# Block-sparse attention with an FFN behind it on one core: who makes the low halves of the weights, and scores of two units in one TensorE task

## The chip, the cores and the metric

The kernel runs on 1 core of one Trainium2 chip. The metric is device time in microseconds (us) of one execution. Engines are named as in the profile: PE is TensorE, PEld its weight loads, DVE is VectorE, ACT is ScalarE, POOL is GpSimd, SP is SyncE, which issues most DMAs.

## The reference

Four batches of eight heads, 768 positions, head dimension 64. Queries and keys are cut into 24 blocks of 32. A query block sees its neighbours, the first and the last block and three sampled blocks; the first and last query block see everything. The result goes through a feed-forward net.

```python
scores = scale * np.matmul(q, k.transpose(0, 1, 3, 2))
mask = np.abs(blk_i - blk_j) <= 1
mask = mask | (blk_i == 0) | (blk_j == 0) | (blk_i == n_blocks - 1) | (blk_j == n_blocks - 1)
...                                     # and three sampled key blocks for each query block
attn = softmax(np.where(mask, scores, -1e9))
x = np.matmul(attn, v)                  # to rows of 512: [3072, 512]
h = x @ w_in                            # [3072, 2048]
out = np.maximum(0.01 * h, h) @ w_out   # [3072, 512]
```

## The kernel before, in words

**Precision.** PE multiplies 16-bit numbers. Every operand is split into a scaled fp16 number (the high half) and an fp16 remainder (the low half), and a product is three matmuls: high by high, high by low, low by high.

**Work.** The 3072 rows are 12 items of 256 rows, three to a batch. An item has four tiles T of 64 queries (two query blocks), and a tile has four units, one for each pair of heads: 192 units, numbered by `u.n`, and two units that follow each other are a pair. A unit goes through: scores (`unit_scores`, L1165, eight matmuls of half-width tiles into one of the two PSUM banks `s`), minimum and mask (`unit_ttr`, L1189, DVE, which frees the bank), exponential (`unit_exp`, ACT), normalising (`pair_norm`, DVE), high half (`unit_high`, ACT, `pp<-p,r`), low half (`unit_split`, DVE, `pp<-p,r,pp`), transposition (`pt<-pp`: by PE for units below 16, by a transposing DMA after that) and the product with the values (`pair_av`, L1245, half-width tiles into the one bank `av`). `tile_evac` (L1263) takes the finished tile out of PSUM: ACT `avt`, DVE `xf`, ACT `x` (high), POOL `x` (low). T = 0 of each batch is the pair of query blocks that see all keys; it has two parts and reads `kt` and `v` directly. The other tiles read gathered copies `kg` (DVE and POOL) and `vg` (DMAs, two of them indirect from POOL).

**FFN.** An item has eight chunks. Chunk: 24 matmuls into one bank `h` (`ffn_h`), ACT `ht<-h` (0.01 h), DVE `ht<-h,ht` (maximum), DVE cast `g<-ht` (high), POOL `g<-ht,g` (low) (`ffn_act1`, `ffn_max`, `ffn_act2`, L1298 to L1311), 12 matmuls into the two banks `o` (`ffn_o`). Items 0 and 1 are "early": they go quarter by quarter, as parts of the weights become ready.

**Weights.** They come as float64 in eight parts: 0, 2, 4, 6 are quarters of `w_in`, 1, 3, 5, 7 quarters of `w_out`. Parts 0 to 5 are handled in two groups of 128x1024 numbers, parts 6 and 7 in four of 128x512. `decode` (L813) makes float32 of the float64 bits: one ACT and three DVE instructions. `finish` (L864) finds one scale for the part (PE squares, DVE), then makes the fp16 halves of each group: ACT the high half, and for the low half the table `wsplit` (L67) says how. With "p" ACT scales the float32 numbers in place and POOL subtracts; with "d" one DVE instruction does both:

```python
nc.scalar.activation(hi, g.d3, AF.Copy, scale=s[:, :1])
if CFG["wsplit"][g.part] == "p":
    nc.scalar.activation(g.d, g.d, AF.Copy, scale=s[:, :1])
    nc.gpsimd.tensor_tensor(out=lo, in0=g.d3, in1=hi, op=ALU.subtract)
else:
    nc.vector.scalar_tensor_tensor(out=lo, in0=g.d3, scalar=s[:, :1], in1=hi, op0=ALU.mult, op1=ALU.subtract)
```

Before, parts 0 to 5 are "p" and 6 and 7 "d".

**Order.** The program is recorded as tasks (class `Plan`, L183). The main loop walks over the units and calls, in the order of the letters in `CFG["ord"]`, the steps of several units; each gets a priority. A planner then plays the tasks through with costs written in `cost` (L466) and fixes one order of instructions for each engine; a `block` of matmuls is one task that nothing comes between. In the running program each engine works strictly in that order and waits on semaphores. All instructions that go through the recording layer carry the profile's line L451 (L461 in the changed kernel), so they are told apart by tile names.

Of the kernel before, what the change touches and what calls it, by code (L numbers as in the profile page):

```python
# [15 lines left out]
F32 = mybir.dt.float32  # L16
# [20 lines left out]
    "pe_t": 16,  # L37
    "passes": 4,
    "stay_ns": 2000.0,
    "kg_dma": 0,  # L40
# [26 lines left out]
    "wsplit": "ppppppdd",  # L67
# [114 lines left out]
class Plan:  # L182
# [283 lines left out]
def cost(eng, method, a, k):  # L466
# [45 lines left out]
def tile_block_sparse_attention_ffn(  # L512
# [69 lines left out]
    group = {"s": banks[:2], "o": banks[2:4], "h": banks[4:7], "av": banks[7:]}  # L582
    turn = dict.fromkeys(group, 0)
# [106 lines left out]
    assert 222 + 2 * P <= DM and 6 + 2 * NB * NR <= 150  # L690
    offs = cst.tile([1, NT - 1, 8], I32, name="offs")
# [3 lines left out]
    lane_m = cst.tile([P, NT - 1, SLOTS], F32, name="maskhalf")  # L695
# [104 lines left out]
    def load_w(g):  # L800
# [12 lines left out]
        def decode():  # L813
# [8 lines left out]
            nc.vector.scalar_tensor_tensor(  # L822
                out=d, in0=hi, scalar=-0x80000000, in1=d, op0=ALU.bitwise_and, op1=ALU.bitwise_or)
# [6 lines left out]
    def prep_weights():  # L830
# [33 lines left out]
        def finish(n, kind, gs):  # L864
            plan.prio = 1000.0 + 200 * CFG["wp"][gs[0].part]
            inv, s = scales(squares([g.d for g in gs], f"{kind}{n}", "w"), 1, f"{kind}{n}", keep=f"{kind}{n}", fl="w")
            invs[kind, n] = inv
            yield 1
            for i, g in enumerate(gs):
# [7 lines left out]
                else:  # L877
                    nc.scalar.activation(hi, g.d3, AF.Copy, scale=s[:, :1])
                    if CFG["wsplit"][g.part] == "p":
                        nc.scalar.activation(g.d, g.d, AF.Copy, scale=s[:, :1])  # L880
                        nc.gpsimd.tensor_tensor(out=lo, in0=g.d3, in1=hi, op=ALU.subtract)
                    else:
                        nc.vector.scalar_tensor_tensor(
                            out=lo, in0=g.d3, scalar=s[:, :1], in1=hi, op0=ALU.mult, op1=ALU.subtract)
                yield g.w
            if kind == "wo":
                pr = cst.tile([P, 1], F32, name=f"pr{n}")
                nc.vector.scalar_tensor_tensor(
                    out=pr, in0=invs["wi", n][:, :1], scalar=1.0 / GDOWN, in1=inv[:, :1], op0=ALU.mult, op1=ALU.mult)
# [30 lines left out]
        done.add("all")  # L920
        yield 1
# [71 lines left out]
    def prep_k(b, hp, rk):  # L993
# [32 lines left out]
        else:  # L1026
            for h in range(2):
                turned("h", kts[b][:, 2 * hp + h, :], k16.rearrange("p n l d -> p (n l d)")[:, h * S:(h + 1) * S],
                       "DVE" if h else "ACT")
# [59 lines left out]
    def gather_k(b, T):  # L1089
# [6 lines left out]
        if n0 < CFG["kg_dma"]:  # L1096
            nc.sync.dma_start(out=kg[:, :, :P], in_=kt[:, :, t0:t0 + P])
# [22 lines left out]
        nc.gpsimd.tensor_copy(  # L1120
# [43 lines left out]
    @levelled(lambda u: u.n + CFG["pr"][0])  # L1164
    def unit_scores(u):  # L1165
        i, c0 = u.k // 2, u.k % 2 * Q2
# [6 lines left out]
        u.nsc = nscale[key]  # L1173
        qs, qxs, _ = qstack[u.b, u.j, i]
# [70 lines left out]
    def pair_av(pr):  # L1245
# [4 lines left out]
        for u in pr.units:  # L1250
            require_v(u.b, u.hp, u.T)
# [78 lines left out]
    def ffn_out(it, t, po, qs):  # L1330
        key = (it.b, "all" if len(qs) == NQ else qs[0])
        if key not in betas:
            betas[key] = cst.tile([P, 1], F32, name=f"beta_{key[0]}_{key[1]}")
            nc.vector.tensor_tensor(out=betas[key], in0=undo[key[1]], in1=vscale[it.b][:, :1], op=ALU.mult)
# [211 lines left out]
    def split_step():  # L1546
        if pend_split:
# [6 lines left out]
            if pu.pi == 1:  # L1554
                pend_av.append((step + CFG["av_lag"], pu.pair))

    def av_step(now=False):
        if pend_av and (now or pend_av[0][0] <= step):
            pr = pend_av.popleft()[1]
            tlive[0] -= 2 * pr.units[0].parts  # L1560
            while evs and pr.hp == 0:
                ev_step()
            pair_av(pr)
            if pr.hp == NP - 2:
                vfree[0] += pr.T > 0
                evs.append((pr.n, tile_evac(pr)))
# [8 lines left out]
    for u in units:  # L1575
# [34 lines left out]
        if step == 0:  # L1610
            unit_scores(u)
        c = aq[0] if aq else None
        for w in CFG["ord"]:
# [7 lines left out]
            elif w == "S" and step + 1 < len(units):  # L1621
                unit_scores(units[step + 1])
# [110 lines left out]
```

## Time and profile before

| what | us |
|---|---|
| median of 3 runs | 844.78 (842.82 to 851.21) |
| the profiled execution's own time | 852.83 |
| its span, first to last instruction | 851.1 |
| PE busy / PEld / DVE / ACT / POOL in the span | 750.1 / 492.0 / 597.5 / 502.5 / 372.3 |

A row of the timeline has start, duration, engine, line, operation, out<-in, shape, count of merged instructions, and in brackets the idle time in front of it and who ended it. Rows of the windows have, for a stretch, the busy time of each engine, the granted PE clock (1.00 is full), and the DMAs' share and rate. A matmul's own duration contains its latency; where many follow each other, the start-to-start distance counts.

### The profile page before, as it was taken

The page shows a single profiled execution, that of the slowest core. Times are in us where ns is not written, and L with a number is a line of the kernel's source. Part 1 is how long each engine was busy: PE and PEld are TensorE (multiplying, and loading weights), DVE is VectorE, ACT ScalarE, POOL GpSimd, SP SyncE. Part 2 cuts the span into 40 slices and gives each one's busy share as a digit, 9 for nine tenths or more (in the row PEclk, how much of TensorE's full clock was granted, in tenths as well). Part 3 has the DMA queues.
Part 4 walks back from the last instruction along what each step waited for, and adds up shares of the span by engine and source line. Part 5 has one row for each costly group of instructions (what it writes and reads, how often), then busy time and mean ns, then how long its engine had stood idle before and what let it go on. Part 6 is the DMA issues. An engine that isn't in the chain of part 4 may idle for free. (4 is left out here: it accounts for less than half of the span.)

```text
span 851.1 us, 19895 instructions
## 1 busy us (share of the span) xinstructions
PE 750.1 (88%) x7204; PEld 492.0 (58%) x7204; DVE 597.5 (70%) x1642; ACT 502.5 (59%) x1087; POOL 372.3 (44%) x558
## 2 busy tenths in 40 slices
PE   3565656688979999999999999999999999979997
PEld 2353445455646656666665666656656666656674
DVE  5897699988768887878867577589587575662221
ACT  6779677566665665757647566476466464552111
POOL 0225457634323555554544446455435364532221
PEclk9567679689989999999999999999999999999999
DMA  9615966598797999999989989789568687591000
GB/s 189 230 39 173 331 149 196 137 192 183 136 150 165 202 206 194 173 213 179 218 163 158 204 152 214 149 160 226 127 130 174 119 157 129 104 165 25 13 14 25
DMA packets 305326, 133.28 MB, mean 157 GB/s; under 512 B 272205, under 2 KB 284621, under 8 KB 305229
## 3 DMA queue, kind: packets, MB, share of 16 engines
q1 hardware_dynamic: 299596, 114.71, 66.9%
q0 software_dynamic: 5632, 17.31, 9.5%
q8 instruction: 56, 0.92, 0.5%
q14 instruction: 42, 0.34, 0.1%
HBM read 65.65 MB, written 12.58 MB: 92 GB/s over the span
## 5 line engine op out<-in xcount | busy, mean ns | idle before, releaser
L451 PE MATMUL h<-x,W 128*128 128x256 f16 x2304 | 285.4, 280 | 8.6 <-ACT x L451 7.8
L451 PEld LDWEIGHTS <-W 128*128 128x128 f16 (+1 forms) x2480 | 240.2, 102 | 80.0 <-issue 24.3
L451 PE MATMUL o<-W,g 128*128 128x512 f16 x1152 | 272.1, 382 | 0.7 <-POOL g L451 0.7
L451 POOL TENSOR_TENSOR g<-ht,g 128x512 f16<-128x512 f32 x96 | 116.8, 1217 | 231.1 <-DVE g L451 182.3
L451 PEld LDWEIGHTS <-g 128*128 128x128 f16 x1152 | 107.4, 99 | 127.2 <-issue 16.6
L451 ACT ACTIVATE p<-p,mx 128x384 f32<-128x384 f32 x208 | 126.0, 607 | 68.8 <-DVE mx L451 66.7
L451 DVE SCALAR_TENSOR_TENSOR pp<-p,r,pp 128x384 f16<-128x384 f32 x208 | 143.4, 721 | 29.3 <-ACT pp L451 27.8
L451 ACT ACTIVATE pp<-p,r 128x384 f16<-128x384 f32 x208 | 117.6, 606 | 34.9 <-issue 11.9
L451 DVE SCALAR_TENSOR_TENSOR ht<-h,gd,ht 128x512 f32<-128x512 f32 x80 | 59.9, 748 | 94.7 <-ACT ht L451 94.3
L451 ACT ACTIVATE ht<-h,gs 128x512 f32<-128x512 f32 x80 | 54.6, 682 | 116.8 <-PE h L451 106.8
L1146 POOL DMA_INDIRECT vg<-scr,vrow x88 | 90.7, 1031 | 70.4 <-PE av L451 49.9
L451 DVE CUSTOM_DVE_ANT_0 p<-s,em,nsc 128x384 f32<-128x384 f32 x176 | 105.3, 609 | 22.7 <-PE s L451 21.5
L1111 POOL COPY kg<-kt 128x128 int32 x264 | 82.3, 348 | 69.2 <-PE s L451 55.3
L451 PE MATMUL av<-pt,vg 128*64 128x128 f16 x2112 | 83.0, 225 | 15.6 <-DMA pt<-pp 8.1
L451 PEld LDWEIGHTS <-vg 128*64 128x64 f16 x2112 | 67.2, 112 | 44.4 <-issue 33.3
L451 PE MATMUL s<-kg,qs 128*64 128x384 f16 x352 | 61.8, 346 | 9.6 <-DVE mx L451 4.2
L451 PE MATMUL s<-kg,qxs 128*64 128x384 f16 x352 | 60.8, 339 | 0.2 <-DMA qxs<-qs 0.2
L451 POOL TENSOR_TENSOR x<-xf,x 128x256 f16<-128x256 f32 x48 | 35.9, 748 | 34.3 <-ACT x L451 32.5
L451 DVE CAST g<-ht 128x512 f16<-128x512 f32 x96 | 42.8, 445 | 10.2 <-PE o L451 7.4
L451 PEld LDWEIGHTS <-qs 128*64 128x64 f16 x416 | 27.7, 113 | 34.9 <-issue 28.5
L451 ACT ACTIVATE avt<-av 128x256 f32<-128x256 f32 x48 | 18.1, 378 | 37.1 <-PE av L451 33.8
L451 ACT ACTIVATION_READ_ACCUMULATOR p<-p,mx 128x1 f32 x208 | 39.3, 189 | 0.0
(127 smaller groups left out, 765.5 us busy)
## 6 DMA issues: line engine op xcount, KB each, us to landing
vg<-scr SPq DMA_DIRECT2D x44, 256.0 KB
v<-in_v_dram SPq DMA_DIRECT2D x32, 192.0 KB
qxs<-qs SPq DMA_DIRECT2D x48, 128.0 KB
scr<-v SPq DMA_DIRECT2D x16, 384.0 KB
rq<-in_q_dram SPq DMA_DIRECT2D x20, 256.0 KB
W<-in_moe_w_in_dram SPq DMA_DIRECT2D x5, 1024.0 KB
out_dram<-ob SPq DMA_DIRECT2D x20, 256.0 KB
rk<-in_k_dram SPq DMA_DIRECT2D x24, 192.0 KB
```

Source lines behind the costliest of these rows:

```text
L451: self.plan.task(self.eng, lambda: f(*a, **k), busy, late, reads, writes, kind, loads, port)
L1111: tc.nc.gpsimd.tensor_copy(out=kg.ap.bitcast(I32)[:, :, slot * BLOCK // 2:(slot + 1) * BLOCK // 2], in_=kt.ap.bitcast(I32)[:, :, bass.ds(o ...
L1146: tc.nc.gpsimd.indirect_dma_start(into.ap, None, scr[b].ap, bass.IndirectOffsetOnAxis(ap=at.ap, axis=0))
```

## The change

1. `wsplit` becomes "ddeeeedd". The low halves of parts 0 and 1 are now made by DVE ("d"). Parts 2 to 5 use a new way "e": a diagonal matrix with the negated scale (`dg`) is made once for a part by ACT; for each 128x512 piece PE multiplies the float32 numbers by it (an f32 matmul) and adds the high half (an fp16 matmul with a unit matrix) in one PSUM bank, and ACT takes the bank out, negated, as the low half. Eight groups of two pieces: 16 such pairs of matmuls. The one bank for it is `h_69` (tag `wl`), taken from the three `h` banks until the last weight is done.
2. The cast `g<-ht` of items 0 and 1 (16 instructions) moves from DVE to ACT (`gact`).
3. From unit 48 on (`pair_at`), and except for T = 0, the scores of both units of a pair are one PE task, and if a `pair_av` is due at that step it is joined to the same task. `pair_av` is one task of 24 matmuls (it was two of 12). From there on a pair's value product comes due 5 steps after its split instead of 3 (`av_lag2`).
4. Small ones: the planner's cost of an f32 matmul is lower; `pr` and `beta` (one column each) are made by `tensor_scalar` instead of two-input forms; the scratch `lane_m` moves into another buffer; other new switches are off.

```diff
-    "wsplit": "ppppppdd",
+    "wsplit": 'ddeeeedd',
+    "pair_at": 48,
+    "join": 1,
+    "av_lag2": 5,
+    "gact": (0, 1),
...
     def block(self, eng="PE"):
+        if self.group is not None:
+            yield
+            return
...
         if lhs.dtype == F32:
-            return 60.0 + 4 * cols, 300.0 + 4 * cols, "f", []
+            return 60.0 + 4 * cols / 2.4, 300.0 + 4 * cols / 2.4, "f", []
...
+    if "e" in CFG["wsplit"]:
+        group["wl"], group["h"] = [group["h"][2]], group["h"][:2]
...
+            if CFG["wsplit"][gs[0].part] == "e":
+                neg = sm.tile([P, 1], F32, tag="neg", name=f"neg_{kind}{n}", bufs=2)
+                nc.vector.tensor_scalar(out=neg, in0=s[:, :1], scalar1=-1.0, scalar2=None, op0=ALU.mult)
...
-                    if CFG["wsplit"][g.part] == "p":
+                    if CFG["wsplit"][g.part] == "e":
+                        if not i:
+                            dg = cst.tile([P, P], F32, tag="dg", name=f"dg_{kind}{n}")
+                            nc.scalar.activation(dg, eye, AF.Copy, scale=neg[:, :1])
+                        for c in range(g.w):
+                            pb = bank("wl", "wl")
+                            with plan.block():
+                                nc.tensor.matmul(pb, dg, g.d3[:, c, :], start=True, stop=False)
+                                nc.tensor.matmul(pb, eye16, hi[:, c, :], start=False, stop=True)
+                            nc.scalar.activation(lo[:, c, :], pb, AF.Copy, scale=-1.0)
+                    elif CFG["wsplit"][g.part] == "p":
...
-        nc.vector.tensor_copy(out=c.g[:, 0], in_=c.t)
+        if c.item.n in CFG["gact"]:
+            nc.scalar.activation(c.g[:, 0], c.t, AF.Copy)
+        else:
+            nc.vector.tensor_copy(out=c.g[:, 0], in_=c.t)
...
+                elif nu.pi == 0:
+                    with plan.level(nu.n + CFG["pr"][0]):
+                        for x in nu.pair.units:
+                            before_scores(x)
+                    due = CFG["join"] and pend_av and pend_av[0][0] <= step
+                    if due:
+                        before_av(pend_av[0][1])
+                    with plan.level(nu.n + CFG["pr"][0]):
+                        with plan.block():
+                            for x in nu.pair.units:
+                                unit_scores(x)
+                            if due:
+                                pair_av(pend_av[0][1])
+                    if due:
+                        after_av(pend_av.popleft()[1])
```

The planner's orders differ nearly everywhere, since it fixes all of them anew. Three places matter below. On POOL, around the second item's first tiles (`x_220` before, `x_222` after, are the item's rows; `vg` gathered values, `offs` block numbers), there stands before:

```order
L451 TENSOR_TENSOR W<-W 128x2x512 x2
L451 TENSOR_TENSOR x_220<-xf,x_220 128x4x64
L1146 DMA vg_90<-scr_71,vrow 128x1024
L451 TENSOR_TENSOR W<-W 128x2x512 x2
L1081 TENSOR_LOAD offs
```

and now:

```order
L461 TENSOR_TENSOR g_217<-ht,g_217 128x512
L1184 DMA vg_89<-scr_71,vrow 64x1024
L1184 DMA vg_89<-scr_71,vrow 128x1024
L461 TENSOR_TENSOR x_222<-xf,x_222 128x4x64
L461 TENSOR_TENSOR g_221<-ht,g_221 128x512
L1114 TENSOR_LOAD offs
```

All twelve subtractions `W<-W` are gone from POOL. On ACT, at the high halves of part 2, there stands before:

```order
L451 ACTIVATE W<-kt_86 128x1024
L451 ACTIVATE W<-W,wi_s 128x2x512 x2
L451 ACTIVATE W<-W,wi_s 128x1024 x2
L451 ACTIVATE W<-W 128x1024
L451 ACTIVATE pp_141<-p_117,r_140 128x384
L451 ACTIVATE pp_142<-p_118,r_140 128x384
L451 ACTIVATE p_133,sum_148<-p_133,mx_119 128x384
L451 ACTIVATE avt<-av_70 128x256
```

and now:

```order
L461 ACTIVATE W<-W,wi_s 128x2x512 x2
L461 ACTIVATE dg<-eye,neg_199 128x128
L461 ACTIVATE p_132,sum_147<-p_132,mx_118 128x384
L461 ACTIVATE W<-W 128x1024
L461 ACTIVATE qa<-rq_106,sc_s_130 128x8x64
L461 ACTIVATE W<-h_69 128x512
L461 ACTIVATE p_133,sum_147<-p_133,mx_134 128x384
L461 ACTIVATE p_116,sum_161<-p_116,mx_144 128x384
L461 ACTIVATE W<-h_69 128x512
L461 ACTIVATE avt<-av_70 128x256
```

The two in-place scalings (`128x1024 x2` from `W,wi_s`) are gone; the pieces that PE has made are taken out one by one (`W<-h_69`) between the exponentials, and the tile's `avt` stands behind two of them. On PE, near unit 98 (first row of each run of matmuls; `s` scores, `av` value products, `h` and `o` FFN), there stands before:

```order
L451 MATMUL h_68<-x_220,W 128x256
...
L451 MATMUL av_70<-pt_143,vg_89 64x128
...
L451 MATMUL s_63<-kg_87,qs_173 64x384
...
L451 MATMUL s_64<-kg_87,qs_173 64x384
...
L451 MATMUL o_65<-W,g_219 128x512
...
L451 MATMUL av_70<-pt_153,vg_90 64x128
```

and now:

```order
L461 MATMUL h_68<-x_222,W 128x256
...
L461 MATMUL s_63<-kg_86,qs_172 64x384
...
L461 MATMUL s_64<-kg_86,qs_172 64x384
...
L461 MATMUL av_70<-pt_158,vg_88 64x128
...
L461 MATMUL av_70<-pt_142,vg_88 64x128
```

Two scores and a whole pair of value products now stand together. Over the whole program the change from full-width to half-width tiles and back happens 151 times in the order before and 121 times in the order now.

More of the change, by code (lines that the diff above doesn't have):

```diff
@@ L37 @@
     "pe_t": 16,
+    "pair_at": 48,
+    "join": 1,
+    "av_lag2": 5,
+    "sign": "dddddddd",
     "passes": 4,
     "stay_ns": 2000.0,
-    "kg_dma": 0,
+    "kg_act": 0,
+    "em_act": 0,
+    "gact": (0, 1),
+    "kt_act": 0,
     "flag": 1,
@@ L821, in decode @@
                 out=d, in0=lo, scalar=29, in1=d, op0=ALU.logical_shift_right, op1=ALU.bitwise_or)
-            nc.vector.scalar_tensor_tensor(
-                out=d, in0=hi, scalar=-0x80000000, in1=d, op0=ALU.bitwise_and, op1=ALU.bitwise_or)
+            if CFG["sign"][g.part] == "p":
+                nc.scalar.activation(hi.bitcast(F32), hi.bitcast(F32), AF.Sign)
+                nc.gpsimd.tensor_tensor(out=f, in0=f, in1=hi.bitcast(F32), op=ALU.mult)
+            else:
+                nc.vector.scalar_tensor_tensor(
+                    out=d, in0=hi, scalar=-0x80000000, in1=d, op0=ALU.bitwise_and, op1=ALU.bitwise_or)
             busy.difference_update(held)
@@ L920, in prep_weights @@
         done.add("all")
+        if "wl" in group:
+            group["h"].extend(group["wl"])
+            turn["h"] = 2 + turn["h"] % 2
         yield 1
@@ L1028, in prep_k @@
                 turned("h", kts[b][:, 2 * hp + h, :], k16.rearrange("p n l d -> p (n l d)")[:, h * S:(h + 1) * S],
-                       "DVE" if h else "ACT")
+                       "DVE" if h and not CFG["kt_act"] else "ACT")
         kready[b, hp] = True
@@ L1162, in levelled, with before_scores @@
         return wrap
-    @levelled(lambda u: u.n + CFG["pr"][0])
-    def unit_scores(u):
-        i, c0 = u.k // 2, u.k % 2 * Q2
+    def before_scores(u):
+        i = u.k // 2
         require_qk(u.b, u.j, i, u.hp)
@@ L1173, in unit_scores @@
         u.nsc = nscale[key]
+    @levelled(lambda u: u.n + CFG["pr"][0])
+    def unit_scores(u):
+        i, c0 = u.k // 2, u.k % 2 * Q2
         qs, qxs, _ = qstack[u.b, u.j, i]
@@ L1554, in split_step @@
             if pu.pi == 1:
-                pend_av.append((step + CFG["av_lag"], pu.pair))
+                pend_av.append((step + CFG["av_lag2" if pu.n >= CFG["pair_at"] else "av_lag"], pu.pair))
     def av_step(now=False):
@@ L1559, in av_step, with before_av, after_av @@
             pr = pend_av.popleft()[1]
[L1560 to L1566, printed above, removed]
+            before_av(pr)
+            with plan.block():
+                pair_av(pr)
+            after_av(pr)
+    def before_av(pr):
+        while evs and pr.hp == 0:
+            ev_step()
+        for u in pr.units:
+            require_v(u.b, u.hp, u.T)
+    def after_av(pr):
+        tlive[0] -= 2 * pr.units[0].parts
+        if pr.hp == NP - 2:
+            vfree[0] += pr.T > 0
+            evs.append((pr.n, tile_evac(pr)))
     def ev_step():
@@ L1610, in tile_block_sparse_attention_ffn @@
         if step == 0:
+            before_scores(u)
             unit_scores(u)
@@ L1621, in tile_block_sparse_attention_ffn @@
             elif w == "S" and step + 1 < len(units):
-                unit_scores(units[step + 1])
+                nu = units[step + 1]
+                if nu.n < CFG["pair_at"] or nu.T == 0:
+                    with plan.level(nu.n + CFG["pr"][0]):
+                        before_scores(nu)
+                    unit_scores(nu)
+                elif nu.pi == 0:
[5 more added lines that the diff above has]
+                        before_av(pend_av[0][1])
+                    with plan.level(nu.n + CFG["pr"][0]):
+                        with plan.block():
+                            for x in nu.pair.units:
[4 more added lines that the diff above has]
+                        after_av(pend_av.popleft()[1])
             elif w == "t":
```

23 lines of the change are left out of this document (15 added, 8 removed).

## The prediction

> **What bounds the kernel now.** I read the page's slices first (PE's busy tenths in 40 slices), then a table of windows by stage, then PE's own timeline.
>
> ```profile
> PE   3565656688979999999999999999999999979997
> 25.00:75.00 50.00, 35.01 (x307) 23.95 (x307) 43.74 (x124) 41.19 (x77) 14.15 (x31) 0.62 0.31 104
> 75.00:125.00 50.00, 25.53 (x277) 18.33 (x278) 37.06 (x75) 35.92 (x66) 30.04 (x32) 0.69 0.89 258
> 100.00:200.00 100.00, 72.57 (x662) 48.47 (x660) 89.85 (x197) 66.13 (x122) 51.49 (x59) 0.81 0.74 181
> 275.00:750.00 475.00, 466.29 (x4722) 302.48 (x4720) 347.71 (x976) 291.32 (x682) 239.99 (x391) 1.00 0.90 171
> ```
>
> Windows list PE, PEld, DVE, ACT, POOL busy, then the clock. There are two programs in one. From 275 us on PE is busy 466.29 of 475 us at full clock: there only fewer or cheaper PE instructions help. Before 225 us PE waits, and runs much of the time at half clock; DVE is nearest to its limit (89.85 of 100 us). Since total PE work is fixed, the end is early PE idle plus lost clock plus PE work. So for each edit I ask: does it change PE's work, or PE's early waits?
>
> PE's longest waits while the weights are made:
>
> ```profile
> 148.78 1.03 PE L451 MATMUL s<-W 128*128 128x128 bf16 x8 [5.14 <-DVE W L451]
> 153.78 0.58 PE L451 MATMUL s<-ssw,ones 128*128 128x1 f32 x2 [1.41 <-DVE s L451]
> 167.85 0.53 PE L451 MATMUL s<-kg,qs 128*64 128x384 f16 x2 [3.17 <-DVE mx L451]
> 168.64 4.36 PE L451 MATMUL h<-x,W 128*128 128x256 f16 x24
> 833.62 2.59 PE o L451 x12
> 836.21 2.62 PE h L451 x24
> ```
>
> DVE ends all three, 9.7 us together. The same 24 matmuls that take 2.62 us late in the program (last row, from the chain of waits) take 4.36 us just after the third wait: a wait is paid twice, the second time in clock.
>
> **The change part by part.**
>
> *POOL loses its twelve weight subtractions.* Why was DVE late? These are DVE rows, then POOL's of the same time:
>
> ```profile
> 79.70 3.26 DVE L451 SCALAR_TENSOR_TENSOR pp<-p,r,pp 128x384 f16<-128x384 f32 x2 [0.93 <-ACT pp L451]
> 114.11 2.47 DVE L451 SCALAR_TENSOR_TENSOR pp<-p,r,pp 128x384 f16<-128x384 f32 x1
> 116.84 1.21 DVE L451 SCALAR_TENSOR_TENSOR W<-W 128x1024 int32<-128x1024 int32 x1
> 123.85 1.14 DVE L451 SCALAR_TENSOR_TENSOR pp<-p,r,pp 128x384 f16<-128x384 f32 x2
> 144.46 4.27 DVE L451 SCALAR_TENSOR_TENSOR W<-W 128x1024 int32<-128x1024 int32 x2
> 148.65 3.05 DVE L451 SCALAR_TENSOR_TENSOR pp<-p,r,pp 128x384 f16<-128x384 f32 x2
> 160.37 6.89 DVE L451 SCALAR_TENSOR_TENSOR W<-kt,W 128x512 int32<-128x512 int32 x3
> 188.36 3.56 DVE L451 SCALAR_TENSOR_TENSOR W<-kt,W 128x512 int32<-128x512 int32 x5
> 144.95 5.77 POOL L451 TENSOR_TENSOR W<-W 128x1024 f16<-128x1024 f32 x2
> 161.41 2.13 POOL L451 TENSOR_TENSOR W<-W 128x1024 f16<-128x1024 f32 x1
> 163.99 2.12 POOL L451 TENSOR_TENSOR W<-W 128x1024 f16<-128x1024 f32 x1 [0.45 <-ACT W L451]
> ```
>
> Five pieces of `W<-kt,W` take 3.56 us (0.71 each); three take 6.89 while POOL subtracts. Two `pp` take 1.14 us undisturbed, and 3.05 and 3.26 beside POOL; one takes 2.47 instead of 0.57; two `W<-W` take 4.27 instead of 2.42 (two of 1.21). The stretching, from 160.37 backwards: 4.8, 1.9, 1.9, 1.9, 2.1: 12.6 us of DVE time, 8.6 of it between 144 and 167 us, in front of PE's three waits. With the subtractions gone I take the waits to go (9.7 us) and the clock loss behind them:
>
> ```profile
> 146.00:156.00 10.00, 5.81 (x31) 4.22 (x32) 9.65 (x16) 7.08 (x13) 8.47 (x9) 0.60 0.24 56
> 163.00:170.00 7.00, 2.67 (x23) 1.56 (x23) 7.00 (x12) 3.30 (x7) 3.47 (x4) 0.65 0.80 217
> ```
>
> PE's busy 5.81 us at 0.60 and 2.67 at 0.65 hold 40% and 35% of loss: 3.3 us. Term: **-13.0**. Bounds: 0 (another late engine takes DVE's place) to -15.9 (all 12.6 us arrive, and the clock). POOL's gathers for `vg` and `kg` no longer stand behind subtractions; no DMA is added or taken away. The Trainium skill ("GPSIMD Engine Reference", Specifications) says that GpSimd shares its SBUF interfaces with VectorE and that instructions with two SBUF inputs contend; the rows above agree.
>
> *PE makes 16 pieces.* No row has an f32 matmul of 512 columns. Nearest:
>
> ```profile
> L451 PEld LDWEIGHTS <-W 128*128 128x128 f16 (+1 forms) x2480 | 240.2, 102 | 80.0 <-issue 24.3
> L451 PEld LDWEIGHTS s<-ssq,ones 128*128 128x128 f32 x48 | 8.9, 211 | 10.8 <-ACT qa L451 6.0 <-issue 2.7 <-DVE r L451 0.5
> L451 PE MATMUL s<-ssq,ones 128*128 128x1 f32 x48 | 8.5, 247 | 6.9 <-ACT qa L451 4.5 <-DVE mx L451 1.8 <-DVE totk L451 0.3
> ```
>
> The program issues 24 such products and the trace has 48: an f32 matmul is two passes. A pass over 512 columns costs at least what an fp16 one does, 2.59/12 = 0.216 us, and an f32 weight load takes 211 ns against 102 for fp16, so I bound a pass by twice that. With the fp16 matmul behind it a piece is 0.65 to 1.08 us; 16 are 10.4 to 17.3. I take the upper end, since f32 showed the factor two where it can be seen. What covers it: in the order all pieces stand between the scores of units 24 and 36, inside 100 to 200 us, where PE is idle 27.4 us; 9.7 of that I have spent above, so 17.7 is left. PE works in order, so I count a third of the pieces as uncovered: **+6.0**; without cover +17.3, and nothing if all is covered. The Trainium skill ("FP8 and Floating Point Precision", TensorE Precision Notes) gives true FP32 four passes: 4 x 0.216 + 0.216 = 1.08 us, my upper end; "Perfetto Trace Analysis" (Engine Utilization) halves the rate for FP32_LOW_HIGH, which makes an estimate of 0.65, my lower one. No run here shows which.
>
> *ACT and DVE trade work.*
>
> ```profile
> L451 ACT ACTIVATE W<-W 128x1024 f32<-128x1024 f32 x9 | 10.1, 1136 | 2.8 <-DVE s L451 2.8
> L451 DVE CAST g<-ht 128x512 f16<-128x512 f32 x96 | 42.8, 445 | 10.2 <-PE o L451 7.4 <-DVE ht L451 0.5 <-issue 0.2
> L451 ACT ACTIVATE qa<-rq 128x512 f16<-128x512 f32 x24 | 14.9, 619 | 4.3 <-DMA qs<-qa 3.5 <-DMA qxs<-qs 0.8
> L451 ACT ACTIVATE ht<-h 128x512 f32<-128x512 f32 x16 | 9.4, 586 | 8.5 <-POOL g L451 6.0 <-PE h L451 2.5
> ```
>
> ACT loses 12 in-place scalings (1.14 each: -13.7) and gains 16 evictions (0.586: +9.4), four `dg` and 16 casts (0.619: +9.9): about +6 us, over a stretch in which it idles 34 of 100 us. That is hidden; without cover it costs 6. What stands behind the evictions on ACT is `avt`, and for that waits the item's FFN: that price is in rival C. DVE loses 16 casts (-7.1 us) in and after the stretch where it is 90% busy; about a quarter should reach PE: **-2.0** (bounds -7.1 and 0). DVE gains four low halves for parts 0 and 1, as long as a `W<-W` of that width (1.21): 4.8 us inside 25 to 100, where it is busy 43.74 of 50 us, then has holes. I take **+2.0** (bounds 0 and 4.8).
>
> *Fewer changes of tile width.* Late in the program:
>
> ```profile
> 735.49 2.75 PE L451 MATMUL o<-W,g 128*128 128x512 f16 x12
> 738.17 0.35 PE L451 MATMUL s<-kg,qs 128*64 128x384 f16 x2
> 738.36 0.33 PE L451 MATMUL s<-kg,qxs 128*64 128x384 f16 x2
> 738.68 0.33 PE L451 MATMUL s<-kg,qxs 128*64 128x384 f16 x2
> 738.94 1.48 PE L451 MATMUL h<-x,W 128*128 128x256 f16 x12
> ```
>
> Twelve `o` matmuls end their turn at 735.49 + 2.59 = 738.08; the half-width scores start at 738.17: 0.09 lost. Scores step by 0.16; the last pair begins at 738.68, so the full-width ones could start at 738.84 and do at 738.94: 0.10 lost. A round trip costs 0.19 us, there are 30 fewer, nearly all in the PE-bound stretch: **-5.7**, hardly hidden by anything.
>
> *The joined tasks' waits.* A pair now needs both `s` banks free and, if joined, both transposed pairs landed; behind it on PE stands the FFN, whose banks ACT and DVE wait for. I cost this at nothing: FFN matmuls of other items stand in front of each pair, and five steps instead of three give the DMAs more time. If that cover failed, a wait as long as one row of scores (0.33 us, above) in front of each of the 66 joined pairs would be 22 us. Gain and loss at the end:
>
> ```profile
> 764.89 0.53 PE L451 MATMUL av<-pt,vg 128*64 128x128 f16 x12 [3.75 <-DMA pt<-pp]
> 784.04 0.39 ACT L451 ACTIVATE avt<-av 128x256 f32<-128x256 f32 x1 [0.84 <-PE av L451]
> 785.00 0.42 ACT L451 ACTIVATE x<-xf 128x256 f16<-128x256 f32 x1 [0.57 <-DVE xf L451]
> 785.78 0.67 POOL L451 TENSOR_TENSOR x<-xf,x 128x256 f16<-128x256 f32 x1
> ```
>
> The 3.75 us should go. But in the order now the last value products have no FFN of the item before behind them: PE waits for `avt`, `xf`, `x`, low `x`, 784.04 to 786.45 less some 0.3 that POOL was held: 2.1 us, and the clock falls again as after the early waits (4.36 - 2.62 = 1.7). Sum **0**; bounds -4 and +4. "TensorE: Matmul & The Clock Gate" of the Trainium skill (HAM oscillation) lets only gaps over about 3.4 us throttle; by that this term would be -1.7.
>
> **Sum:** -13.0 + 6.0 - 2.0 + 2.0 - 5.7 + 0 = -12.7 us, made against the profiled execution's own 852.83 (span 851.1 and 1.7 around it): 840.1. That execution is 8 us over the median, 844.78, so I put the same difference there: **832.1**.
>
> **The rivals.**
> - *A, DVE sets the early pace:* DVE's 12.6 us of stretching and 7.1 of casts, less 4.8 for parts 0 and 1, all arrive (14.9), PE's pieces are hidden, clock and tile changes add 3.3 and 5.7: -23.9, **821**. For it: DVE 89.85 of 100 us. Against it: PE also waits for ACT and DMAs there.
> - *B, the relief goes to waste:* another wait takes over and PE's pieces fill the idle time; only the tile changes count: -5.7, **839**. For it: the early order is new, and PE's waits before had many causes.
> - *C, slower: PE and ACT in lock step over one bank.* A piece can start only when ACT has emptied `h_69` of the one before, and ACT, in order, has up to three pieces of 0.6 in front. PE, in order, holds FFN and scores meanwhile, and `avt` stands behind the evictions. With 1.7 us a piece: 27.2 + 17.3 - 17.7 = 26.8, 3 for clock, 2 for parts 0 and 1, less 13.0, 2 and 5.7: +11, **856**. It decides from about 1.5 us a piece on. Against it: ACT idles a third of that time, and other work stands between most pieces.
>
> **How the numbers follow.** Chances: forecast 0.40 (its own range 824 to 839), A 0.22, B 0.24, C 0.14. About 1%, 836.3 to 853.2, is what a measurement can tell from no change. Faster: A, most of the forecast (0.36) and a little of B (0.06): 0.64. Same: the rest of these, 0.22. Slower: C, 0.14. The range goes from 810, below A, to 851; about 0.15 lies above it.
>
> **What would show it.** Right: no DVE row of one or two inputs over 1.5 times its undisturbed length between 130 and 170; PE's waits for `W` and `mx` there gone; clock over 0.9 in 140 to 175; pieces of about 1.1 us on PE; PE's sum over the late stretch shorter by 5 to 6 us. Wrong: PE waiting for ACT before `dg` matmuls (C); PE's busy share in 275 to 750 below 97%, with waits for `mx` before scores (the joined task is not free).

## The result and the profile after

The changed kernel takes **820.6 us** (median of 4 runs, 817.98 to 822.22), the kernel before on the same chip 843.8 (842.11 to 851.21): a ratio of 0.971, 95% interval 0.964 to 0.977. The forecast was 832.1, with 810 to 851 as its range. The direction and the range hold; the gain is twice the one forecast. A second comparison on another chip gave 0.969 (0.965 to 0.973), 824.0 against 849.7. The chips used here put the kernel before anywhere between 843.8 and 852.9, so from here on only ratios to the kernel before on the same chip are compared, and "us" of a gain is such a ratio times 850.

PE's slices and its clock, from the page of the changed kernel:

```profile
PE   3566789998899999999999999999999999999997
PEclk9986689999999999999999999999999999999999
```

PE's tenths reach 9 in the seventh slice (123 us) and stay at 8 or more until the last; before, they do so from the thirteenth (255 us), but for one 7 in the thirty-sixth. The same windows as in the prediction (PE, PEld, DVE, ACT, POOL busy, clock, DMA):

```profile
25.00:75.00 50.00, 31.61 (x288) 22.54 (x286) 42.73 (x115) 38.17 (x69) 7.68 (x22) 0.80 0.31 102
75.00:125.00 50.00, 38.90 (x373) 25.03 (x373) 39.38 (x100) 38.92 (x76) 26.60 (x41) 0.76 0.90 260
100.00:200.00 100.00, 89.40 (x798) 54.45 (x796) 83.84 (x219) 77.36 (x154) 40.92 (x59) 0.96 0.90 207
146.00:156.00 10.00, 9.55 (x96) 5.39 (x93) 7.53 (x24) 8.80 (x18) 3.62 (x7) 1.00 0.54 118
163.00:170.00 7.00, 6.55 (x45) 3.44 (x42) 6.02 (x22) 5.38 (x12) 1.16 (x1) 1.00 1.18 147
275.00:750.00 475.00, 468.47 (x4805) 318.36 (x4803) 346.66 (x962) 295.79 (x684) 232.54 (x377) 1.00 0.86 170
```

Read alone, the third row tells the story that the prediction hoped for: PE busy 89.40 us of 100 instead of 72.57, at 0.96 of the clock instead of 0.81. But busy time at a high clock is not yet progress: 17 us of it are the pieces that PE did not have to do before.

So I measured **progress** from the matmuls themselves. Late in the program a matmul of `h` costs 0.109 us start to start, one of `o` 0.2165, a score matmul 0.080 (two in 0.16), a value matmul 0.0295; the products that started before 275 us, times these, are the useful PE work done by then. For the second profiles of both kernels, taken beside experiments on chips where the kernel before took 850 us:

| | before | changed | saved, us |
|---|---|---|---|
| `h`, `o`, score, value matmuls begun before 275 us | 420, 177, 248, 648 | 432, 200, 248, 672 | |
| useful PE work done by 275 us | 123.1 | 130.1 | 7.0 |
| changes of tile width after 275 us, at 0.095 | 210 | 150 | 5.7 |
| PE idle after 275 us | 17.5 | 8.4 | 9.1 |
| what is left (steps longer than these prices, at half clock for instance) | 13.0 | 8.6 | 4.4 |
| span | 847.6 | 822.0 | 25.6 |

(Idle is the sum of the times from the end of one matmul to the start of the next. The four sum to 26.2, by which PE's last matmul ends earlier; what stands behind that matmul takes 0.6 us longer.) In this pair of profiles a fourth of the gain is made early. More than half, 13.5 us, is idle time and longer steps in the stretch that the prediction called bound by PE, and for which it had forecast nothing but the 5.7 us of tile widths. The first pair of profiles shares the gain out otherwise: 19.5 us early (115.6 and 135.1 done by 275 us), 6.7 in tile widths, 5.1 in idle time (13.5 and 8.4) and 2.3 in what is left, of 33.0 us between the spans, 10 us more than between the medians of these runs. So the early share, 7.0 to 19.5 us, is not settled by two pairs; idle time and longer steps after 275 us fell in both, by some 7 and by 13.5 us.

What PE waits for after 275 us (total us, times, longest; first rows), first before, then changed, second profiles:

```profile
PE av L451 <- DMA pt<-pp: 8.6, 7, 3.6
PE s L451 <- DVE mx L451: 3.6, 4, 1.5
PE s L451 <- DVE r L451: 2.4, 2, 1.4
PE s L451 <- DVE s L451: 1.3, 3, 0.8
```

```profile
PE s L461 <- DVE s L461: 1.9, 4, 0.7
PE s L461 <- DVE mx L461: 1.5, 2, 0.9
PE h L461 <- ACT x L461: 1.4, 1, 1.4
PE s L461 <- DVE r L461: 1.3, 3, 0.6
```

The waits of value products for transposed pairs are gone altogether, not only the 3.75 us near the end that the prediction saw.

### The profile page after: what moved, and what is told of

Read it like the earlier page. It is cut to its first block, busy times and chain, and to the rows that moved or that the text cites. A ratio compares the mean times of both kernels' runs of the same rounds, so it can differ in the third digit from the quotient of the medians.

```text
span 818.1 us, 19976 instructions
## 1 busy us (share of the span) xinstructions
PE 749.7 (92%) x7252; PEld 502.5 (61%) x7252; DVE 582.4 (71%) x1634; ACT 511.3 (62%) x1111; POOL 342.9 (42%) x546
## 5 line engine op out<-in xcount | busy, mean ns | idle before, releaser
L461 PE MATMUL h<-x,W 128*128 128x256 f16 x2304 | 272.7, 274 | 4.6 <-DVE ht L461 1.7
L461 PEld LDWEIGHTS <-W 128*128 128x128 f16 (+1 forms) x2480 | 237.0, 100 | 61.8 <-issue 16.5
L461 PE MATMUL o<-W,g 128*128 128x512 f16 x1152 | 265.2, 379 | 0.1
L461 PEld LDWEIGHTS <-g 128*128 128x128 f16 x1152 | 109.6, 98 | 120.6 <-issue 3.7
L461 DVE SCALAR_TENSOR_TENSOR pp<-p,r,pp 128x384 f16<-128x384 f32 x208 | 135.2, 679 | 24.6 <-ACT pp L461 23.5
L1184 POOL DMA_INDIRECT vg<-scr,vrow x88 | 87.3, 992 | 84.5 <-PE av L461 69.3
L1144 POOL COPY kg<-kt 128x128 int32 x264 | 87.7, 369 | 81.5 <-PE s L461 66.0
L461 PEld LDWEIGHTS <-vg 128*64 128x64 f16 x2112 | 69.8, 113 | 14.9 <-issue 7.7
L461 PE MATMUL av<-pt,vg 128*64 128x128 f16 x2112 | 76.3, 225 | 2.0 <-DMA vg<-scr,vrow 0.9
L461 DVE CAST g<-ht 128x512 f16<-128x512 f32 x80 | 35.2, 440 | 8.7 <-PE o L461 6.8
```

The lines of the kernel that those rows point to most:

```text
L461: self.plan.task(self.eng, lambda: f(*a, **k), busy, late, reads, writes, kind, loads, port)
L1144: tc.nc.gpsimd.tensor_copy(out=kg.ap.bitcast(I32)[:, :, slot * BLOCK // 2:(slot + 1) * BLOCK // 2], in_=kt.ap.bitcast(I32)[:, :, bass.ds(o ...
L1184: tc.nc.gpsimd.indirect_dma_start(into.ap, None, scr[b].ap, bass.IndirectOffsetOnAxis(ap=at.ap, axis=0))
```

## The experiments

Theories at the start: *relief* (POOL's subtractions held DVE up, and the relief reaches the end whole, as in rival A), *size on record* (the prediction's terms for the weights hold, the surplus is the pairing's), and *pieces* (PE's pieces fill its holes and hold its clock up). The expectations in us for `zero_p`, `all_d`, `only_w` and `back_p` are against 843.8; on the chip of these runs before took 852.2, so 826 reads 0.979, 831 reads 0.985.

### Relief of DVE and the price of the pieces, with the order kept

**zero_p.** The kernel before, instruction for instruction, but for POOL; in effect:

```diff
-nc.gpsimd.tensor_tensor(out=lo, in0=g.d3, in1=hi, op=ALU.subtract)
+nc.gpsimd.memset(lo, 0.0)        # issued at the place planned for the subtraction
```

> The kernel before, with every engine's order kept instruction for instruction, but each POOL subtraction that makes a low half of weight parts 0 to 5 is replaced by a POOL write of zeros to the same place (the low halves of these parts are left out of the product). Three theories of the 23 us. Relief: POOL's two-input work stretched DVE, PE waited for DVE and lost clock, and the relief also reaches the stretch after 200 us, so it alone is worth about 18 us: 826. Size on record: the relief is worth the 13.0 us of the prediction and the rest comes from the pairing of the scores: 831. Pieces: what helps is that PE has work of its own in its holes, which keeps its clock up: without the pieces 840 or more. In the first two DVE has no row over 1.5 times its undisturbed length in 144 to 167 us; in the first PE's idle time in 117 to 275 us falls from 25.6 us to below 12.

Measured: 0.9905 (0.987 to 0.994), 8 us. The contention was real. DVE's rows of the same place, where two `W<-W` took 4.27 us beside a subtraction:

```profile
143.40 2.46 DVE L454 SCALAR_TENSOR_TENSOR W<-W 128x1024 int32<-128x1024 int32 x2
145.77 0.64 DVE L454 SCALAR_TENSOR_TENSOR pp<-p,r,pp 128x384 f16<-128x384 f32 x1
146.79 1.31 DVE L454 SCALAR_TENSOR_TENSOR pp<-p,r,pp 128x384 f16<-128x384 f32 x1 [0.37 <-ACT pp L454]
```

The last of them is still 2.3 times its undisturbed 0.57 us: POOL's subtraction for `g` (146.53, 1.16 us), which this edit leaves in, runs beside it. And PE's idle time in 117 to 275 us only fell from 27.3 us (23.8 in the second profile of before) to 19.3, not below 12. 12.6 us of DVE time became 8 us of the end. Relief falls, and the prediction's 13.0 was too large.

**zero_pair.** The same edit in the order with pairing, old weight table and DVE casts (`only_pair` below).

> The kernel with pairing and lag of 5 but the old weight table and the casts on DVE (0.988 of before), every engine's order kept, with POOL's twelve subtractions replaced by writes of zeros (the low halves of parts 0 to 5 are left out). In the order of before the same edit was worth 8 us at the end, though 12.7 us more of PE's work was done by 275 us: 4.6 us went into waits after that. Theory given back late: with pairing and lag of 5 there are few waits after 275 us for it to be lost in, so it arrives whole: 12 to 14 us, 0.972 to 0.974. Rival, 8 us everywhere: 0.978. Rival, DVE is not what bounds this order: 0.985 or more.

Measured: 0.981 (0.976 to 0.986) against 0.988 (0.982 to 0.993): 6 us, about as large as the uncertainty of the two ratios, with idle time after 275 us unchanged (9.2 and 9.0). So the relief is 8 us in the one order and some 6 in the other, and "given back late", which expected 12 to 14, falls.

**cheap_e** and **twice_e.** The changed kernel's order, with the piece's f32 product cheaper or done twice; in effect:

```diff
-nc.tensor.matmul(pb, dg, g.d3[:, c, :], start=True, stop=False)
+nc.tensor.matmul(pb, eye16, hi[:, c, :], start=True, stop=False)      # cheap_e
...
 nc.tensor.matmul(pb, dg, g.d3[:, c, :], start=True, stop=False)
+nc.tensor.matmul(pb, dg, g.d3[:, c, :], start=False, stop=False)      # twice_e
```

> The changed kernel with every engine's order kept, but the f32 product of each of the 16 pieces is an fp16 product of the same 128x512 (the low halves of parts 2 to 5 are then not the remainder, so that part of the computation is left out). A piece costs 0.43 us instead of 1.08, 10.4 us less PE work in all. The prediction's third uncovered: 3.5 us faster than the changed kernel. Pieces all in idle time: the same within 1 us. Nothing covered: 10 us faster. Pieces hold the clock up: slower by 2 us or more, with a granted clock below 0.95 in 117 to 225 us.

> The changed kernel with every engine's order kept, and each of the 16 f32 products done twice into the same bank (the low halves of parts 2 to 5 then contain the product twice, so that part of the computation is changed): 16 x 0.86 = 13.8 us more PE work in 100 to 170 us. Half of a piece's price shows, as when it was made cheaper: 7 us, 0.977. The prediction's third: 4.6 us, 0.975. All of it, since no idle time is left to hide more: 14 us, 0.986.

Measured: 0.964 (0.960 to 0.968) beside 0.969 for the changed kernel, 5.2 us of 10.4 by the medians on one chip; and 0.981 (0.975 to 0.987), 10 us of 13.8. Between the two ends 24.2 us of PE work cost 0.0172, 14.6 us: **0.6 of each us of a piece arrives at the end**. For the 17.2 us that the 16 pieces take, that makes about 10 us, an estimate that goes beyond the two ends. They do not pay by holding the clock.

**all_d** (`wsplit` "dddddddd": DVE makes all low halves) and **half_pieces** ("ddeedddd": eight pieces).

> The changed kernel with all low halves by DVE: POOL is as free as in the changed kernel, PE makes no pieces, ACT takes no pieces out, DVE has eight more subtractions of 1.2 us (about 10 us). Relief: DVE is what is short, so some of its 10 us come back as PE's waits: 826 to 830. Size on record: the pieces cost 6 us and a fifth to a third of DVE's 10 us shows: 818. Pieces: without them PE's holes and the low clock return: 832 or more, with PE idle time in 117 to 225 us above 20 us.

> The changed kernel with PE making the low halves of parts 2 and 3 only (8 pieces instead of 16) and DVE those of 4 and 5. Half of a piece's price showed at the end when the pieces were made cheaper, so 8 pieces of 1.08 us are worth 4 us; DVE's four subtractions more cost 1 to 2 us: 0.966 to 0.968, a little faster than the changed kernel. If a new order's luck decides: 0.963 to 0.976.

Measured: 0.968 (0.961 to 0.974) and 0.967 (0.963 to 0.972), both level with the changed kernel (0.971 and 0.969 in its two comparisons). DVE's extra subtractions and PE's pieces cost about the same here. In 117 to 225 us stand `all_d` and then the changed kernel's second profile:

```profile
117.00:225.00 108.00, 86.48 (x840) 58.35 (x839) 96.60 (x265) 74.40 (x154) 41.24 (x61) 0.89 0.88 188
```

```profile
117.00:225.00 108.00, 96.93 (x895) 61.52 (x893) 90.69 (x246) 80.70 (x166) 43.56 (x62) 0.98 0.87 182
```

PE is busy 10 us longer and at a clock of 0.98 instead of 0.89, and yet 85.0 and 82.4 us of useful work are done by 225 us, 130.8 and 130.1 by 275 us (88.1 and 135.1 in the changed kernel's first profile). The low clock that `pieces` expected did come, but the time did not. That theory falls.

### The weight table alone

**only_w** (the kernel before with the new table; the pairing, the lag and the casts put back) and **back_p** (the changed kernel with "ppppppdd").

> The kernel before with the new weight table alone: no pairing, no joined tasks, the lag of value products at 3 again, first casts on DVE. Relief: keeps all but the 5.7 us of fewer width changes and 2 us of casts: 828. Size on record: 13 - 6 - 2 = 5 us gained, so 839, and the pairing holds the rest. Pieces: 828 as well.

> The changed kernel with only the weight table put back: POOL subtracts for parts 0 to 5 again, and PE makes no pieces; pairing and casts stay as changed. Relief: loses about 18 us, 838, and DVE rows beside POOL are long again. Size on record: loses 13 - 6 = 7 us, 828. Pieces: 838 too, but with a granted clock in 117 to 225 us that is low although DVE is no later than in the changed kernel.

Measured: 0.986 (0.979 to 0.993) and 0.973 (0.966 to 0.979). Putting the table back costs the changed kernel only 0.003, 3 us. So with the other edits in place the largest edit by its text is worth next to nothing (6 to 8 us of relief against 10 us of pieces would even make it a small loss, which the uncertainty of the ratios allows), and the surplus has to be elsewhere. But `only_w` is faster by more than its terms. It shares a thing with the changed kernel that I had not priced by itself, the one PE task of 24 matmuls for a pair's value products.

### The one task of 24 matmuls

**av24.** The kernel before with the changed kernel's way of letting one `block` stand inside another, and

```diff
...
-            pair_av(pr)
+            for u in pr.units:
+                require_v(u.b, u.hp, u.T)
+            with plan.block():
+                pair_av(pr)
```

> The kernel before with one edit: the value products of a pair are one PE task of 24 matmuls instead of two of 12. In the order 202 changes of tile width are left of 302. Theory block: this edit alone, which the prediction did not price by itself, holds much of the surplus: 100 changes fewer at 0.095 us are 9.5 us, and the waits that stood between the halves go, so 0.982 to 0.989 of before. Theory joined: the paired scores and the longer lag hold the rest, so fewer changes without them bring at most the 0.99 that the changes are worth. Theory early: width changes and waits of value products lie in idle time, and the early stage decides: 0.995 to 1.005.

**all_off.** The changed kernel with table, pairing, lag and casts put back.

> The changed kernel with its weight table, its pairing with lag and its first casts on ACT all put back: only the one task of 24 matmuls for a pair's value products and the small edits are left; 222 changes of tile width. Block: 80 changes fewer, 7.6 us, and the waits: 0.983 to 0.991. Joined: 0.99 to 1. Early: 1.

Measured: 0.991 (0.988 to 0.994), 7.6 us for 100 fewer changes of width, where 9.5 was worked out; and 0.983 (0.979 to 0.988), 14 us. The first agrees with the price of a change of width (its interval is 5 to 10 us), and this edit alone brings more of them than the whole change does (202 left, against 242). What the other 6.5 us of `all_off` are, I can't say: of the small edits, which the prediction put at nothing, none was run alone, and its order is a new one too.

### Pairing and lag

**no_pair** (scores unpaired, nothing joined, lag 3), **only_pair** (all put back but pairing and lag), **lag5_only** (lag 5 without pairing), **pair_lag3** and **lag4** (pairing with lag 3 and 4):

```diff
-    "pair_at": 48, "join": 1, "av_lag2": 5,
+    "pair_at": 10 ** 9, "join": 0, "av_lag2": 3,       # no_pair; lag5_only: a lag of 5 from unit 48 on
...
-    "av_lag2": 5,
+    "av_lag2": 3,                                      # pair_lag3; lag4: 4
```

> The changed kernel without the pairing of scores, without joined tasks and with the lag of value products at 3 again; weight table, casts on ACT and the one task of 24 matmuls stay; 230 changes of tile width. Theory pairing: the 9 us that lie between the kernel with all four switches put back (0.983 of before) and the one with only the weight table put back (0.973) are the pairing's: 0.979 to 0.981. Theory casts: they are the casts': 0.969. Theory order: each edit makes the planner fix a new order, whose luck is worth some 4 us either way; then single edits do not add up, and this one may come out on either side of 0.975.

> The kernel with all four switches put back, plus the pairing of scores, the joined tasks and the lag of 5 alone (POOL subtracts, DVE casts). Theory pairing: 0.983 less 9 us, 0.973 to 0.975. Theory casts: 0.983. In the first PE's idle time after 275 us falls below 9 us and waits for value products there vanish.

> The changed kernel without paired scores and joined tasks, but with the lag of 5 for value products from unit 48 on. Theory lag: the longer lag alone takes the waits after 275 us away (20.3 us without pairing and with lag 3, 8.4 in the changed kernel): 0.970 to 0.975. Theory together: the paired scores hold half of it: 0.978 to 0.982. Theory pairing: 0.985 to 0.989.

> The changed kernel with the lag of value products at 3 instead of 5 from unit 48 on; scores stay paired and joined. If the longer lag holds the pairing's gain, since PE then no longer waits for transposed pairs: 0.977 to 0.981, with 5 us or more of idle time in front of value products after 275 us. If the paired scores hold it: 0.969 to 0.971.

> The changed kernel with the lag of value products at 4 instead of 5 from unit 48 on; scores stay paired; 234 changes of tile width. With 3 the paired scores gave 0.997, with 5 they give 0.969. Theory room: a whole pair of scores needs both score banks at once, and one step more is what the minimum and the other DVE steps between need; at 4 half of it is there: 0.980 to 0.986, idle time after 275 us 14 to 20 us. Theory threshold: 4 is enough: 0.969 to 0.973, idle time after 275 us below 10 us. Theory luck: lag 3 met one bad place in its order (5.9 us and the clock behind it), not a trend: below 0.975 as well, but with the waits spread otherwise.

| pairing | lag | ratio (95%) | work done by 275 us | PE idle after 275 us |
|---|---|---|---|---|
| no (no_pair) | 3 | 0.987 (0.981 to 0.993) | 134.8 | 20.3 |
| no (lag5_only) | 5 | 0.986 (0.981 to 0.991) | 129.8 | 18.7 |
| yes (pair_lag3) | 3 | 0.997 (0.993 to 1.001) | 134.9 | 26.1 |
| yes (lag4) | 4 | 0.970 (0.965 to 0.976) | 131.9 | 10.0 |
| yes (changed) | 5 | 0.969 (0.965 to 0.973) | 130.1 | 8.4 |

This is the surplus: **15 us, and in these orders it comes only with both**. The longer lag without pairing brings nothing, the pairing with the old lag loses 9 us, and from lag 4 on the two together bring it. It lies after 275 us. That the fewer waits are not the luck of one order, the profiles of all runs show: with pairing and a lag of 4 or 5 PE is idle for 6.4 to 10.0 us after 275 us in all eleven (seven orders), without pairing for 11.0 to 20.5 us in all eight (six orders). `no_pair` waits there for (first rows):

```profile
PE s L461 <- DVE mx L461: 6.2, 9, 0.7
PE av L461 <- DMA pt<-pp: 3.4, 2, 2.9
```

Nine waits for `mx`, nearly all of one length. One of them, in its timeline:

```profile
688.36 0.35 PE L461 MATMUL s<-kg,qs 128*64 128x384 f16 x2
...
688.87 0.33 PE L461 MATMUL s<-kg,qxs 128*64 128x384 f16 x2
689.03 0.84 PE L461 MATMUL av<-pt,vg 128*64 128x128 f16 x24
690.59 0.35 PE L461 MATMUL s<-kg,qs 128*64 128x384 f16 x2 [0.71 <-DVE mx L461]
```

and DVE beside it:

```profile
689.25 0.75 DVE L461 SCALAR_TENSOR_TENSOR ht<-h,gd,ht 128x512 f32<-128x512 f32 x1 [4.00 <-ACT ht L461]
689.92 0.61 DVE L461 CUSTOM_DVE_ANT_0 p<-s,em,nsc 128x384 f32<-128x384 f32 x1
690.45 0.08 DVE L461 DVE_READ_ACCUMULATOR2_ANT mx<- 128x1 f32 x1
```

Two units fill both score banks, one pair of value products follows, and the third unit's scores stand there before DVE has freed a bank, since an FFN maximum (`ht`) came first. In the changed kernel the same pattern stands like this (second profile):

```profile
705.61 0.35 PE L461 MATMUL s<-kg,qs 128*64 128x384 f16 x2
...
706.28 1.51 PE L461 MATMUL av<-pt,vg 128*64 128x128 f16 x48
707.62 0.33 PE L461 MATMUL s<-kg,qs 128*64 128x384 f16 x2
...
708.11 0.33 PE L461 MATMUL s<-kg,qxs 128*64 128x384 f16 x2
708.37 2.79 PE L461 MATMUL h<-x,W 128*128 128x256 f16 x24
```

Two pairs of value products (1.34 us) stand between the two pairs of scores, and DVE is through in time. That longer lag is what has two pairs of values ready to stand there fits the table, but is argued, not shown. With lag 3, `pair_lag3` waits 11.0 us for `r` instead, and half of that in one place, where PE stands before the sum of squares of the next keys (`ssk`) and half clock follows:

```profile
317.85 0.35 PE L461 MATMUL s<-ssq,ones 128*128 128x1 f32 x2 [0.36 <-DVE mx L461]
324.12 0.56 PE L461 MATMUL s<-ssk,ones 128*128 128x1 f32 x2 [5.92 <-DVE r L461]
324.54 2.72 PE L461 MATMUL h<-x,W 128*128 128x256 f16 x12
```

(12 `h` matmuls take 1.48 us at full clock.) So a part of its loss is one unlucky place, and lag 4 does not tell a threshold from luck. Without that place 20.2 us of its idle time would still be left, as many as `no_pair` has: the pairing alone would not have brought the gain either.

`only_pair` came out at 0.988 (0.982 to 0.993), *not* below `all_off` (0.983): with the old table and DVE casts the pairing brings nothing. There PE was idle only 11.0 us after 275 us without pairing, and 9.0 with it, so there was little to remove. Why the planner's order of `no_pair` has 20.3 us of idle time there and that of `all_off` 11.0 stays open. Table and casts without pairing do 9.8 us more by 275 us (134.8 against 125.0) and lose 9.3 in idle time after it.

So what pairing is worth hangs on the table and the casts, and what these are worth on the pairing. Put side by side, the runs show it (all have the one task of 24 and the small edits; "pairing" includes the lag of 5):

| weight table | casts on ACT | without pairing | with pairing |
|---|---|---|---|
| old | no | 0.983 (all_off) | 0.988 (only_pair) |
| new | no | 0.986 (only_w) | 0.974 (no_gact) |
| old | yes | not run | 0.973 (back_p) |
| new | yes | 0.987 (no_pair) | 0.969 (changed) |

With pairing either the table alone or the casts alone brings 12 to 13 us, and the second of them only 3 to 4 more; without pairing the table brings nothing, nor do table and casts together. Both take work that stretches DVE or stands on it out of the early stage. That the time won there is kept only where few waits are left after 275 us would fit these numbers, but is argued, not shown.

The switch `join` itself does nothing: with it off the planner's orders of all five engines are the same, row for row. The places where paired scores and value products stand together are the planner's.

### Casts, and the two controls

**no_gact** (the first casts on DVE again), **after_again** and **before_again** (both kernels once more):

> The changed kernel with the 16 first casts on DVE again. Theory pairing: the casts are worth what the prediction gave them, 2 us: 0.972. Theory casts: DVE is short in the early stage and takes back 7.1 us of casts: 0.978 to 0.981, with PE's idle time in 117 to 275 us up by 6 us or more.

> The changed kernel once more, beside the others on one chip: all theories expect 0.97 of the kernel before.

> The kernel before once more, for a second profile of its early and late stages: 1.00. If the first profile is typical, the work that PE has done by 275 us agrees within 6 us (115.6) and the idle time after it within 3 us (13.5).

Measured: 0.974 (0.969 to 0.979), 4 us less than the changed kernel, with idle time in 117 to 275 us up by 1 to 3 us only; 0.969; 1.002 (0.999 to 1.005). The difference of 4 us is about as large as the uncertainty of two ratios. With the old table the same casts are worth 13 us (`back_p` against `only_pair`, 0.973 and 0.988).

### A better version

None is found. `all_d` and `half_pieces` equal the changed kernel within their intervals, and `cheap_e`, the one below it, does not make the low halves.

## Why the prediction was off, step by step

- **What bounds the kernel.** "From 275 us on ... only fewer or cheaper PE instructions help": this sentence failed, and with it the forecast. PE's 466.29 busy us of 475 looked full, but that window hides what ends after 750 us and the small waits: in the two profiles of before 13.5 and 17.5 us of idle time and some 13 us in longer steps stood after 275 us, and the change took some 7 and 13.5 us of these away.
- **The joined tasks' waits, at nothing.** This step failed most: it asked what a pair's longer needs would cost, and never what the longer lag would free, apart from the 3.75 us near the end. Measured: 15 us gained by pairing and lag together, with table and casts in place (0.987 to 0.969). By which path the lag frees them is argued above, not shown. The 66 joined pairs that it counted are not made by the joining.
- **The terms as a sum.** Each edit got a price of its own, and the prices were added. With pairing the casts are worth 13 us or 4 and the table 12 or 3, as the other is missing or there; without pairing the table is worth nothing. No sum of fixed prices gives that.
- **POOL's subtractions, -13.0.** Too large: -6 to -8, by the same order with zeros written. Of the 12.6 us of DVE time about 60% arrived.
- **The pieces, +6.0.** Too small: about +10, since not a third but 0.6 of their time showed. Their length was right. The pieces in the changed kernel by their tile: the f32 products, 32 records for 16, with their durations, and PE's wait for `dg` (us, times); PE's waits for ACT's `W` in 117 to 225 us; then one piece in the timeline:

```profile
L461 PE MATMUL h<-W,dg x32: 592/594/1222, 107.0 to 159.8; 128*128 128x512 f32 x32
...
  PE h L461: 1.9, 1
```

```profile
PE h L461 <- ACT W L461: 1.4, 4, 0.7
```

```profile
154.04 0.86 PE L461 MATMUL av<-pt,vg 128*64 128x128 f16 x24
154.83 1.13 PE L461 MATMUL h<-W,dg 128*128 128x512 f32 x2
155.79 0.38 PE L461 MATMUL h<-W,eye 128*128 128x512 f16 x1
```

  From the first pass to the fp16 matmul 0.96 us, of which 0.10 is the change from half-width tiles; that leaves 0.43 for each of two passes, and with 0.216 for the fp16 matmul 1.08 us, the upper end of the bounds. Four fp16 matmuls of that width would take 0.86 us, so the four passes of true FP32 in the Trainium skill ("FP8 and Floating Point Precision", TensorE Precision Notes) agree with it, and the halved rate that its "Perfetto Trace Analysis" (Engine Utilization) gives for FP32_LOW_HIGH does not.
- **Casts, -2.0; low halves of parts 0 and 1, +2.0.** The first measured at -4, uncertain, with the new table and at -13 with the old; the second was not run alone.
- **Changes of tile width, -5.7.** Right within the uncertainty: 60 fewer, all after 275 us, and 100 fewer by themselves gave 7.6 us (5 to 10) where the price gives 9.5.
- **The end, 0.** The 3.75 us went, and the new wait came, smaller than worked out: 1.39 and 0.48 us.
- **The small edits, not priced.** They and their new order may hold up to 6.5 us (`all_off` against `av24`), left open.
- **The rivals.** A's 821 is the time that came, but not for its reason: DVE's relief did not arrive whole. C's lock step did not come: in front of the pieces PE waited 1.9 us for `dg` and 1.4 for `W` (rows above), 3.3 us over 16 pieces or 0.2 for each, where C had reckoned 1.7 beside the piece itself.
- **What would show it.** Four DVE rows between 130 and 170 us are still over 1.5 times their length (2.05 and 2.17 for 1.21, 1.02 for 0.57, 1.38 for 0.74), beside POOL's `g` and `x`: 2.9 us in place of the 8.6 that the prediction found between 144 and 167 us. PE's waits for DVE's `W` are gone, and the clock in 140 to 175 us is 1.00. A sign of being wrong came too, PE's waits for ACT before `dg` products, but small (3.3 us). Most signs were near what was forecast and none of them told where the gain was, because none looked past 275 us for waits that go.

In order of the kernels run, the gain is: one task of 24, 7.6 us; small edits and a new order, 6.5; table and casts, -3 (0.983 to 0.987); pairing with lag, 15: 26 in all. The steps are not additive. Taken the other way round from `all_off` on, pairing with lag is worth -4 (0.983 to 0.988), the casts then 13 (0.973) and the table 3. So no one of the three holds the surplus; the runs show it where pairing with lag stands together with the table or the casts.

## What to carry to other kernels

An engine that is busy 98% of a window still has waits: here these and the longer steps gave some 7 us in one pair of profiles and 13.5 in the other. List them before calling the engine full, and take two profiles of each kernel before sharing a gain out. Measure progress in finished useful work at a fixed time, not in busy time or clock: added work raises both and moves nothing. Where a planner fixes the order anew, an edit of a few lines can be worth as much as the relief of an engine (0.991 for the one task of 24, 0.9905 for the zeros), so price each edit by a run that keeps the order where one can be made. And run edits with and without each other: here the same casts were worth 4 us or 13.

## What the hardware showed unexpectedly

- **The same wait, with and without half clock.** The changed kernel's wait of 1.39 and 0.48 us near the end, in its first and second profile:

```profile
768.96 0.27 PE L461 MATMUL h<-x,W 128*128 128x256 f16 x1 [1.39 <-ACT x L461]
769.71 9.58 PE L461 MATMUL h<-x,W 128*128 128x256 f16 x71 [0.48 <-POOL x L461]
```

```profile
774.48 0.27 PE L461 MATMUL h<-x,W 128*128 128x256 f16 x1 [1.38 <-ACT x L461]
775.23 7.91 PE L461 MATMUL h<-x,W 128*128 128x256 f16 x71 [0.48 <-POOL x L461]
```

  The same 71 matmuls take 9.58 and 7.91 us: in the first, 15 of them step by 213 ns instead of 109 before the full step returns (so the clock price at the end, worked out as 1.7 us, came once and once not). The Trainium skill ("TensorE: Matmul & The Clock Gate", Part 1) describes an activity window of about 3.4 us that runs freely, without regard to the kernel's start; 15 steps of 213 ns and the two mixed ones beside them (148 and 173) are 3.5 us, which agrees. Its rule of thumb (HAM oscillation) that PE's gaps should stay under about 3.4 us is not enough here: shorter ones sufficed, in one execution of two.
- **Who waits for whom depends on POOL's operation.** In `zero_p` POOL's copies for `kg` ran twice like this, the second time beside DVE's two `W<-W` of 143.40 (2.46 us, their undisturbed length, against 4.27 beside a subtraction):

```profile
136.43 0.77 POOL L1114 COPY kg<-kt 128x128 int32 x3
...
143.56 3.00 POOL L1114 COPY kg<-kt 128x128 int32 x3 [0.45 <-DVE r L454]
```

  Beside POOL's two-input subtraction DVE is stretched; beside its copies with one input DVE keeps its length and POOL takes four times as long (so again in this run at 109.31 us: 3.21 us for three copies, beside two `W<-kt,W` of 2.50 us in all).
